# Weight remainders of the expert stage: three quarters on VectorE, one quarter on GpSimd, and two weight loads released from a wait

## The chip, the cores and the metric

The kernel runs on one core of one Trainium2 chip. The metric is the device time of one execution in microseconds (us); the medians here are over a few executions of the same program. A core has TensorE (PE in the rows; PEld is its weight load), VectorE (DVE), ScalarE (ACT), GpSimd (POOL) and SyncE (SP), each with its own queue that is worked off strictly in order; they wait for one another by semaphores. SP issues most DMAs, POOL issues the indirect ones (gathers and scatters).

## The reference

Three layers run one after the other: an attention with heads mixed before and after the softmax, a dense layer, and a layer of eight experts with one expert per token. The change lies in the third.

```
xn = x / (norm(x) + 1e-6); en = expert_emb / (norm(expert_emb) + 1e-6)
logits = xn @ en.T / tau
expert_idx = argmax(logits, axis=1)          # 1792 tokens, 8 experts
gate_w = softmax(logits)[token, expert_idx]
for e in range(8):
    mask = expert_idx == e
    h = maximum(x[mask] @ w1[e], 0)          # 768 -> 1024
    out[mask] = gate_w[mask] * (h @ w2[e])   # 1024 -> 768
```

Everything is float32 in and out.

## The kernel before

Products are made from 16-bit pieces: a float32 operand is split into a high part (float16) and a remainder (bfloat16, the float32 value less its high part), and three matmuls (high by high, remainder by high, high by remainder) are added up in PSUM.

**The expert stage** (`moe2`, `one_round`) goes through nine lists of tokens. List 0 holds the first 276 tokens of the fullest expert and starts while the dense layer is still ending; lists 1 to 7 hold the other experts, at most 306, 276, 224, 208, 208, 192 and 160 tokens; list 8 is the rest of the fullest expert, 64 tokens. A list is eight units. For unit (e, f) one DMA of 768 KB brings a tile `wr` with 128 rows of the first weight (j = 0) and of the second (j = 1), out of six buffers (`fetch`, L870 to L876). `split` (L892 on) makes the high part `wh` on ScalarE (L902) and the remainder `wl` (L903), 128x768 each; these have three buffers for each j. `first` multiplies the list's tokens with the first weight (18 matmuls, L913), applies the relu (ScalarE writes `rh`, L917; VectorE writes `rl` from PSUM, L918); `second`, two units later, multiplies with the second weight (18 matmuls, L937). After a list's last unit its sums are copied out (`ot`, L947 on VectorE and L949 on ScalarE), transposed on TensorE (L966), scaled by the gate (`or`, L971, VectorE) and scattered to the output by GpSimd (L974).

The tokens of a list come as rows: SP loads the list's indices `ids` (L833), GpSimd gathers the rows `xr` out of the DRAM table `yg` (L839), TensorE transposes them (L854), ScalarE and VectorE write the two pieces `xph` (L858) and `xpl` (L859, from PSUM). The gather for list e+1 is issued at unit (e, 0). These transposes, the units' first products and the output transposes take turns in two PSUM banks.

**Between dense layer and list 1** stands the routing of the last 256 tokens: their sums are copied (`yt`, L569), logits taken, the expert picked and placed (L598 to L648), the rows normalised and written to `yg` (L698), the counts of the experts ranked (L725 to L739). Only then can list 1 be gathered. List 0's remainders are kept for list 8 (`kept_xl`, the same line L903), so list 8 needs none.

**The order.** Lines are written in the order of the loops; a scheduler that follows dependencies moves them on each engine's queue. SP issues the weight DMAs ahead as far as `PF` = 5 units reach and buffers are free; the DMA of unit (1, 0) waits besides, by a dependency written by hand (L873), until the gathered rows of list 1 have landed, and SP being in order, those of (1, 1) and so on stand behind it.

Of the kernel before, what the change touches and what calls it, by code (L numbers as in the profile page):

```python
# [17 lines left out]
ALU = mybir.AluOpType  # L18
# [782 lines left out]
def moe2(tc, ctx, bank, ident, yg, pos, keep, ids0, chosen, w12, out, before):  # L801
    nc = tc.nc
# [22 lines left out]
    def one_round(lists, wins, offs, nm, before=None):  # L825
# [44 lines left out]
        def fetch(e, f):  # L870
            raw = p4.tile([128, 2, DM], F32, tag="wr", name=f"wr_{nm}_{e}_{f}")
            s = nc.sync.dma_start(out=raw, in_=w12[bass.ds(lists[e][0], 1), f].rearrange("o p j d -> (o p) j d"))
            if before and (e, f) == (1, 0):  # L873
                tc.add_manual_dep(s.ins, gathered[-1].ins.name,
                                  mybir.DependencyInfo(mybir.DependencyClass.Sync, mybir.DependencyReason.DATA),
                                  reason="the gathered rows are needed before these weights")  # L876
            for j in range(2):
                RW[e, f, j] = raw[:, j]

        def lasting(f, j):  # L880

            if (f, j) not in kept:
                p, n = (chosen["pool"], 4) if f < 4 else (late["w"], 2 * MF - 8)
                t = [p.tile([128, CC, 512] if f < 4 else [128, n * DM], dt, tag=tag, name=f"kept_{tag}_{f}")
                     for dt, tag in ((F16, "xh"), (BF, "xl"))]
                if f < 4:
                    t = [x.rearrange("p a b -> p (a b)") for x in t]
                for k in range(n):
                    kept[f + k // 2, k % 2] = tuple(x[:, k * DM:(k + 1) * DM] for x in t)
            return kept[f, j]  # L890

        def split(e, f, j):  # L892
            if wins[e] == LATE:
                RW[e, f, j] = kept[f, j]
                return
            raw = RW[e, f, j]
            if before and e == 0:
                wh, wl = lasting(f, j)
            else:
                wh = p3.tile([128, DM], F16, tag=f"wh{j}", name=f"wh{j}_{nm}_{e}_{f}")  # L900
                wl = p3.tile([128, DM], BF, tag=f"wl{j}", name=f"wl{j}_{nm}_{e}_{f}")
            nc.scalar.copy(wh, raw)  # L902
            (nc.vector if j else nc.gpsimd).tensor_tensor(out=wl, in0=raw, in1=wh, op=ALU.subtract)  # L903
            RW[e, f, j] = (wh, wl)

        def first(e, f):
# [76 lines left out]
        def fetch_to(i):  # L983
            while ahead and units.index(ahead[0]) <= i and ahead[0][0] < len(lists):
                fetch(*ahead.pop(0))

        fetch_to(0)
        gather(0, *((ids0, 1 + BLOCKS[-1][0]) if before else ()))
        fetch_to(PF - 1)
        split(0, 0, 0)  # L990
        split(0, 0, 1)
        for c in range(3):
            if before:
# [5 lines left out]
        for i, (e, f) in enumerate(units):  # L999
# [3 lines left out]
            if i + 1 < len(units):  # L1003
                with ExitStack() as order:
                    if before and i < 3:
                        order.enter_context(tc.issue_after(chosen["hl" if i < 2 else "rows"].ins))
                    split(*units[i + 1], 0)
                    split(*units[i + 1], 1)
# [145 lines left out]
```

## Time and profile before

| | us |
|---|---|
| median of 3 executions (lowest, highest) | 1286.94 (1285.57, 1294.75) |
| the profiled execution, its own time | 1288.26 |
| its span, first to last instruction | 1286.0 |
| TensorE busy in the span | 1193.8 |
| VectorE, ScalarE, GpSimd busy | 855.1, 729.0, 707.3 |
| expert stage, lists 1 to 8 and the end | about 1029 to 1286 of the span |

How to read it: all times in the rows are counted from the start of the span. "Busy" is the time in which an engine has an instruction running, including time for which that instruction is held up. A share over the whole span mixes three layers; the rows that follow are therefore cut by stretches.

### The profile page before, as it was taken

Reading aid. Unit: us, or ns where it says so; the run is one execution under the profiler, and the core shown is the slowest. Engines: PE = TensorE matmul, PEld = TensorE weight load, DVE = VectorE, ACT = ScalarE, POOL = GpSimd, SP = SyncE. Lnnn points to the kernel's source line nnn. Section 1 sums busy time; section 2 is a strip of 40 time slices with the busy share of each in tenths; the row PEclk is TensorE's granted clock in tenths of the full one; section 3 lists DMA queues with packets and bytes.
Section 4 is the critical chain, followed back from the end, with each engine's and each line's share of the span. In section 5 each row is a group of like instructions: output and inputs, shape, how many; then the busy total and the mean of one; then the engine's idle time right before and its main releaser. Section 6 shows DMA issues by size and latency. Waiting matters only on the chain.

```text
span 1286.0 us, 23742 instructions
## 1 busy us (share of the span) xinstructions
PE 1193.8 (93%) x8624; PEld 837.4 (65%) x8648; DVE 855.1 (66%) x1895; ACT 729.0 (57%) x1499; POOL 707.3 (55%) x594
## 2 busy tenths in 40 slices
PE   8999899989999988999899999999978899999995
PEld 3655565555555664566566666667876678989883
DVE  5877687768767829977766456745878345566662
ACT  6777687667767744444455444545556334555551
POOL 5887678577767753433443335334566355566550
PEclk8999999999999999999999999999998999999998
DMA  6555746555574476223001000100043656678640
GB/s 212 174 182 146 221 162 190 175 182 184 148 208 162 116 236 219 93 97 131 25 1 50 1 25 1 50 1 1 2 140 133 212 194 205 213 242 263 229 159 22
DMA packets 82854, 173.90 MB, mean 135 GB/s; under 512 B 12155, under 2 KB 60155, under 8 KB 82728
## 3 DMA queue, kind: packets, MB, share of 16 engines
q1 hardware_dynamic: 76986, 160.75, 38.7%
q0 software_dynamic: 5472, 11.43, 3.0%
q8 instruction: 70, 1.15, 0.4%
q14 instruction: 56, 0.46, 0.1%
q10 hardware_dynamic: 270, 0.12, 0.0%
HBM read 110.79 MB, written 23.30 MB: 104 GB/s over the span
## 4 chain that ended last, share of the span: by engine, by line
PE 59%; DVE 16%; DMA 12%; ACT 6%; issue 3%; POOL 2%; SPq 0%; POOLq 0%; ACTq 0%; DVEq 0%
PE bank L561 11%; PE bank L533 10%; PE bank L913 7%; PE bank L240 7%; PE bank L937 7%; PE bank L290 7%; DMA G<-S 3%; PE bank L203 3%; DMA raw_v<-in_v_dram 3%; PE bank L305 2%; DVE g L547 2%; DMA wor<-in_w_out_dram 2%; DVE g L548 2%; DVE wl_a L903 2%; ACT A L250 1%
## 5 line engine op out<-in xcount | busy, mean ns | idle before, releaser
L561 PE MATMUL bank<-ghl,whl 128*128 128x512 f32 (+1 forms) x1152 | 258.1, 376 | 9.3 <-POOL ghl L551 4.9
L561 PEld LDWEIGHTS bank<-ghl,whl 128*128 128x128 f32 x1152 | 199.6, 192 | 50.8 <-POOL ghl L551 6.3
L483 POOL TENSOR_TENSOR whl<-wo,whl 128x768 fp32r<-128x768 f32 x64 | 118.8, 1857 | 177.2 <-ACT whl L482 177.1
L295 POOL TENSOR_TENSOR at<-at 128x480 f16<-128x480 f32 x180 | 177.0, 996 | 51.9 <-ACT at L294 50.2
L240 PE MATMUL bank<-G,wmix 120*120 120x448 f32 x360 | 176.7, 575 | 11.3 <-DMA G<-S 11.3
L290 PE MATMUL bank<-wr,A 120*128 120x120 f32 (+4 forms) x1800 | 175.3, 246 | 5.2 <-ACT x L312 3.0
L250 ACT ACTIVATE A<-bank,st 120x448 f32<-120x448 f32 x180 | 114.3, 636 | 53.5 <-DVE st L244 22.2
L244 DVE TENSOR_REDUCE st<-bank 120x1 f32<-120x448 f32 x180 | 111.2, 618 | 46.3 <-PE bank L240 45.1
L903 POOL TENSOR_TENSOR wl_a<-wr_a,wh_a 128x768 bf16<-128x768 f32 x56 | 93.1, 1670 | 70.4 <-ACT wh_a L902 70.0
L551 POOL TENSOR_TENSOR ghl<-g,ghl 128x512 fp32r<-128x512 f32 (+1 forms) x64 | 76.6, 1197 | 99.7 <-ACT ghl L550 99.7
L903 DVE TENSOR_TENSOR wl_a<-wr_a,wh_a 128x768 bf16<-128x768 f32 x56 | 83.1, 1484 | 61.9 <-ACT wh_a L902 61.9
L533 PEld LDWEIGHTS <-wih 128*128 128x128 f16 x768 | 72.4, 99 | 76.3 <-issue 15.9
L290 PEld LDWEIGHTS bank<-wr,A 120*128 120x128 f32 (+1 forms) x720 | 94.5, 198 | 34.5 <-issue 17.8
L294 ACT COPY at<-bank 128x480 f32<-128x480 f32 x180 | 101.3, 567 | 25.0 <-PE bank L290 24.7
L902 ACT CAST wh_a<-wr_a 128x768 f16<-128x768 f32 x112 | 92.6, 829 | 39.2 <-PE bank L937 35.2
L543 DVE SCALAR_TENSOR_TENSOR g<-bank,u 128x512 f32<-128x512 f32 (+1 forms) x64 | 39.9, 623 | 108.6 <-ACT d L540 105.2
L255 POOL TENSOR_TENSOR A<-A 120x448 f16<-120x448 f32 (+1 forms) x90 | 84.4, 938 | 32.0 <-ACT A L250 13.4
L482 ACT CAST whl<-wo 128x768 fp32r<-128x768 f32 x64 | 53.1, 831 | 71.1 <-PE bank L561 53.0
L533 PE MATMUL bank<-mxh,wih 128*128 128x512 f16 (+1 forms) x384 | 85.1, 358 | 5.4 <-DVE d L544 4.2
L290 PEld LDWEIGHTS <-A 120*128 120x128 bf16 (+2 forms) x1080 | 63.1, 100 | 40.9 <-issue 33.9
L550 ACT CAST ghl<-g 128x512 fp32r<-128x512 f32 (+1 forms) x64 | 36.2, 566 | 91.6 <-DVE g L548 81.0
L913 PE MATMUL bank<-xph_a,wh_a 128*128 128x208 f16 (+5 forms) x336 | 87.2, 262 | 0.0
(214 smaller groups left out, 2701.3 us busy)
## 6 DMA issues: line engine op xcount, KB each, us to landing
wr_a<-in_w_dram SPq DMA_DIRECT2D x64, 768.0 KB
G<-S SPq DMA_DIRECT2D x176, 210.0 KB
raw_w<-in_w_in_dram SPq DMA_DIRECT2D x32, 384.0 KB
wor<-in_w_out_dram SPq DMA_DIRECT2D x16, 768.0 KB
raw_v<-in_v_dram SPq DMA_DIRECT2D x16, 384.0 KB
yg<-row SPq DMA_DIRECT2D x3, 1540.0 KB
raw_q<-in_q_dram SPq DMA_DIRECT2D x9, 448.0 KB
raw_k<-in_k_dram SPq DMA_DIRECT2D x9, 448.0 KB
```

What stands on the lines that cost most here:

```text
L240: nc.tensor.matmul(ps[:r, :S], wmix[:r, :r], g[:r], start=True, stop=True)
L244: nc.vector.tensor_reduce(out=st[:r, k:k + 1], in_=ps[:r, :S], axis=AX.X, op=ALU.min)
L250: nc.scalar.activation(out=a[:r, :S], in_=ps[:r, :S], func=AF.Exp, bias=bias, scale=-1.0, accum_out=st[:r, 4 + k:5 + k])
L290: nc.tensor.matmul(ps[:, jc * r:jc * r + r], x[:r, js], w[:r].rearrange("p (a b) -> p a b", b=10)[:, :, :n], start=(i == 0), stop=(i == le ...
L294: nc.scalar.copy(at32[:, :, t0:t0 + n], v)
L295: nc.gpsimd.tensor_tensor(out=atl[:, :, t0:t0 + n], in0=at32[:, :, t0:t0 + n], in1=ath[:, :, t0:t0 + n], op=ALU.subtract)
L483: nc.gpsimd.tensor_tensor(out=w[:, 1], in0=wo[f], in1=w[:, 0].bitcast(F32), op=ALU.subtract)
L533: nc.tensor.matmul(h, u[f][:, c], X[b][v][:, c, :N], start=(i == 0), stop=(i == len(seq) - 1))
L561: nc.tensor.matmul(Y[b][c][:, :N], w[:, u, 128 * c:128 * c + 128], hl[:, v, :N], start=(f == 0 and i == 0), stop=(f == FC - 1 and i == 2))
L902: nc.scalar.copy(wh, raw)
L903: (nc.vector if j else nc.gpsimd).tensor_tensor(out=wl, in0=raw, in1=wh, op=ALU.subtract)
L913: nc.tensor.matmul(h, w[u][:, 128 * c:128 * c + 128], XP[e][v][:, c, :N], start=(i == 0), stop=(i == len(seq) - 1))
```

## The change

The remainders were made on VectorE for the second weight (j = 1) and on GpSimd for the first (j = 0). Now GpSimd makes them where f + 2j is a multiple of four: the first weight of units 0 and 4 and the second weight of units 2 and 6, four of a list's sixteen; VectorE makes the other twelve. The dependency on the gathered rows moves from the DMA of unit (1, 0) to that of unit (1, 2).

```diff
@@ fetch
-            if before and (e, f) == (1, 0):
+            if before and (e, f) == (1, 2):
                 tc.add_manual_dep(s.ins, gathered[-1].ins.name,
@@ split
             nc.scalar.copy(wh, raw)
-            (nc.vector if j else nc.gpsimd).tensor_tensor(out=wl, in0=raw, in1=wh, op=ALU.subtract)
+            (nc.gpsimd if (f + 2 * j) % 4 == 0 else nc.vector).tensor_tensor(out=wl, in0=raw, in1=wh, op=ALU.subtract)
```

The scheduler's queues change at these places. In the names, `wl0_a_4_3` is the remainder of the first weight (j = 0) of list 4, unit 3; `xr_a_5_0` is a third or half of list 5's rows.

GpSimd's queue about the gather for list 5, which is issued while list 4 begins; before:

```order
L903 TENSOR_TENSOR wl0_a_4_1_13046<-wr_a_4_1_12794,wh0_a_4_1_13045 128x768
L903 TENSOR_TENSOR wl0_a_4_2_13097<-wr_a_4_2_12862,wh0_a_4_2_13096 128x768
L839 DMA xr_a_5_0_13041<-yg_61,ids_a_5_13039 104x770
L839 DMA xr_a_5_1_13043<-yg_61,ids_a_5_13039 104x770
L903 TENSOR_TENSOR wl0_a_4_3_13161<-wr_a_4_3_12920,wh0_a_4_3_13160 128x768
L903 TENSOR_TENSOR wl0_a_4_4_13232<-wr_a_4_4_12986,wh0_a_4_4_13231 128x768
L903 TENSOR_TENSOR wl0_a_4_5_13291<-wr_a_4_5_13037,wh0_a_4_5_13290 128x768
L974 DMA out_0_dram<-or_a_3_0_13152,oi_a_3_0_12479 1792x768
```

and now:

```order
L903 TENSOR_TENSOR wl0_a_4_0_12989<-wr_a_4_0_12729,wh0_a_4_0_12988 128x768
L903 TENSOR_TENSOR wl1_a_3_6_12869<-wr_a_3_6_12594,wh1_a_3_6_12868 128x768
L839 DMA xr_a_5_0_13041<-yg_61,ids_a_5_13039 104x770
L839 DMA xr_a_5_1_13043<-yg_61,ids_a_5_13039 104x770
L903 TENSOR_TENSOR wl0_a_4_4_13232<-wr_a_4_4_12986,wh0_a_4_4_13231 128x768
L903 TENSOR_TENSOR wl1_a_4_2_13101<-wr_a_4_2_12862,wh1_a_4_2_13100 128x768
L974 DMA out_0_dram<-or_a_3_0_13152,oi_a_3_0_12479 1792x768
L974 DMA out_0_dram<-or_a_3_1_13223,oi_a_3_1_12483 1792x768
```

Behind the gather stand two remainders instead of three before the scatter, and one of the two belongs to the second weight.

VectorE's queue at the same place, from the relu remainder `rl` of unit (4, 1) on; before:

```order
L918 SCALAR_TENSOR_TENSOR rl_a_4_1_13124<-bank7_828_13104,rh_a_4_1_13123 128x208
L947 COPY ot_a_3_13145<-bank1_810_12700 128x224
L947 COPY ot_a_3_13145<-bank3_812_12702 128x224
L947 COPY ot_a_3_13145<-bank5_814_12704 128x224
L971 TENSOR_SCALAR or_a_3_0_13152<-bank6_829_13153,gate_a_3_0_12478 112x384
L903 TENSOR_TENSOR wl1_a_4_2_13101<-wr_a_4_2_12862,wh1_a_4_2_13100 128x768
L918 SCALAR_TENSOR_TENSOR rl_a_4_2_13188<-bank7_830_13168,rh_a_4_2_13187 128x208
L971 TENSOR_SCALAR or_a_3_0_13152<-bank6_831_13191,gate_a_3_0_12478 112x384
```

and now:

```order
L918 SCALAR_TENSOR_TENSOR rl_a_4_1_13124<-bank7_828_13104,rh_a_4_1_13123 128x208
L947 COPY ot_a_3_13145<-bank1_810_12700 128x224
L947 COPY ot_a_3_13145<-bank3_812_12702 128x224
L947 COPY ot_a_3_13145<-bank5_814_12704 128x224
L971 TENSOR_SCALAR or_a_3_0_13152<-bank6_829_13153,gate_a_3_0_12478 112x384
L918 SCALAR_TENSOR_TENSOR rl_a_4_2_13188<-bank7_830_13168,rh_a_4_2_13187 128x208
L971 TENSOR_SCALAR or_a_3_0_13152<-bank6_831_13191,gate_a_3_0_12478 112x384
L903 TENSOR_TENSOR wl0_a_4_5_13291<-wr_a_4_5_13037,wh0_a_4_5_13290 128x768
```

The remainder that stood ahead of `rl` of unit (4, 2) is gone from VectorE; the next one stands behind it.

VectorE's queue between list 0 and list 1, from `rl` of unit (0, 4) to the fourth of the six pieces `xpl` of list 1; before:

```order
L918 SCALAR_TENSOR_TENSOR rl_a_0_4_11300<-bank6_745_11280,rh_a_0_4_11299 128x276
L918 SCALAR_TENSOR_TENSOR rl_a_0_5_11347<-bank7_746_11327,rh_a_0_5_11346 128x276
L918 SCALAR_TENSOR_TENSOR rl_a_0_6_11394<-bank6_747_11374,rh_a_0_6_11393 128x276
L859 TENSOR_TENSOR xpl_a_1_11398<-bank7_748_11399,xph_a_1_11397 128x306
L903 TENSOR_TENSOR wl1_a_1_0_11436<-wr_a_1_0_11225,wh1_a_1_0_11435 128x768
L859 TENSOR_TENSOR xpl_a_1_11398<-bank6_749_11423,xph_a_1_11397 128x306
L903 TENSOR_TENSOR wl1_a_1_1_11531<-wr_a_1_1_11274,wh1_a_1_1_11530 128x768
L918 SCALAR_TENSOR_TENSOR rl_a_0_7_11459<-bank7_750_11439,rh_a_0_7_11458 128x276
L859 TENSOR_TENSOR xpl_a_1_11398<-bank6_751_11462,xph_a_1_11397 128x306
L903 TENSOR_TENSOR wl1_a_1_2_11582<-wr_a_1_2_11321,wh1_a_1_2_11581 128x768
L859 TENSOR_TENSOR xpl_a_1_11398<-bank7_752_11486,xph_a_1_11397 128x306
```

and now:

```order
L918 SCALAR_TENSOR_TENSOR rl_a_0_4_11300<-bank6_745_11280,rh_a_0_4_11299 128x276
L903 TENSOR_TENSOR wl1_a_1_0_11436<-wr_a_1_0_11225,wh1_a_1_0_11435 128x768
L918 SCALAR_TENSOR_TENSOR rl_a_0_5_11347<-bank7_746_11327,rh_a_0_5_11346 128x276
L903 TENSOR_TENSOR wl0_a_1_1_11527<-wr_a_1_1_11274,wh0_a_1_1_11526 128x768
L903 TENSOR_TENSOR wl1_a_1_1_11531<-wr_a_1_1_11274,wh1_a_1_1_11530 128x768
L918 SCALAR_TENSOR_TENSOR rl_a_0_6_11394<-bank6_747_11374,rh_a_0_6_11393 128x276
L859 TENSOR_TENSOR xpl_a_1_11398<-bank7_748_11399,xph_a_1_11397 128x306
L903 TENSOR_TENSOR wl0_a_1_2_11578<-wr_a_1_2_11321,wh0_a_1_2_11577 128x768
L859 TENSOR_TENSOR xpl_a_1_11398<-bank6_749_11423,xph_a_1_11397 128x306
L918 SCALAR_TENSOR_TENSOR rl_a_0_7_11459<-bank7_750_11439,rh_a_0_7_11458 128x276
L859 TENSOR_TENSOR xpl_a_1_11398<-bank6_751_11462,xph_a_1_11397 128x306
L859 TENSOR_TENSOR xpl_a_1_11398<-bank7_752_11486,xph_a_1_11397 128x306
```

Of the three remainders that stood among the pieces `xpl` one is left; three others stand ahead of them.

On SP's queue nothing changes its place: the write of `yg`, the indices of list 1, then the DMAs of units (1, 0), (1, 1), (1, 2), of which the third now carries the wait for the rows.

## Rows read from the trace of the kernel before

**Rows 1.** The page, busy us of each engine, share of the span, instructions.

```profile
PE 1193.8 (93%) x8624; PEld 837.4 (65%) x8648; DVE 855.1 (66%) x1895; ACT 729.0 (57%) x1499; POOL 707.3 (55%) x594
```

**Rows 2.** Busy time by stretch: length, each engine's us and (count), granted clock, DMA share, GB/s.

```profile
1015.00:1029.00 14.00, 11.03 (x80) 8.55 (x81) 7.84 (x9) 6.95 (x13) 5.39 (x3) 0.88 0.92 366
1029.00:1140.00 111.00, 111.00 (x982) 95.49 (x981) 58.41 (x107) 53.19 (x94) 60.01 (x40) 1.00 0.64 210
1140.00:1256.00 116.00, 107.24 (x1215) 104.61 (x1213) 77.44 (x116) 62.61 (x115) 67.91 (x44) 0.97 0.66 215
```

**Rows 3.** The same by stretches of 4 us, inside lists 4 to 7.

```profile
1148.00:1152.00 4.00, 1.20 (x12) 1.05 (x12) 3.89 (x5) 0.78 (x1) 2.08 (x3) 1.00 0.17 45
1208.00:1212.00 4.00, 1.53 (x9) 1.43 (x10) 3.62 (x5) 0.15 (x1) 2.07 (x2) 0.82 0.21 30
1212.00:1216.00 4.00, 4.00 (x38) 3.88 (x37) 1.68 (x3) 1.14 (x3) 0.97 (x2) 0.75 0.93 339
1232.00:1236.00 4.00, 2.43 (x29) 2.04 (x26) 4.00 (x3) 2.62 (x7) 2.70 (x2) 1.00 0.28 51
1236.00:1240.00 4.00, 3.19 (x28) 3.10 (x29) 3.47 (x9) 1.02 (x2) 0.00 (x0) 0.74 0.91 350
1240.00:1244.00 4.00, 4.00 (x48) 3.98 (x47) 2.04 (x5) 1.52 (x3) 2.59 (x2) 0.84 0.20 55
```

**Rows 4.** Waits of TensorE from 920 us on: us in total, times, longest.

```profile
PE bank L966 <- DVE rl_a L918: 6.1, 3, 3.1
...
PE bank L854 <- DMA xr_a<-yg,ids_a: 3.2, 3, 1.3
PE bank L854 <- DVE xpl_a L859: 3.2, 3, 1.6
PE bank L966 <- DVE ot_a L947: 2.3, 1, 2.3
```

**Rows 5.** Timeline of GpSimd at list 4: start, us, what.

```profile
1144.77 4.86 POOL L903 TENSOR_TENSOR wl_a<-wr_a,wh_a 128x768 bf16<-128x768 f32 x3
```

**Rows 6.** Timeline of VectorE at the same place.

```profile
1141.61 0.96 DVE L903 TENSOR_TENSOR wl_a<-wr_a,wh_a 128x768 bf16<-128x768 f32 x1 [1.74 <-ACT wh_a L902]
...
1145.03 5.42 DVE L903 TENSOR_TENSOR wl_a<-wr_a,wh_a 128x768 bf16<-128x768 f32 x1
```

**Rows 7.** Line L903 in the whole span: ns shortest/median/longest, first and last start.

```profile
L903 POOL TENSOR_TENSOR wl_a<-wr_a,wh_a x56: 1637/1647/2173, 1020.1 to 1247.7; 128x768 bf16<-128x768 f32 x56
L903 DVE TENSOR_TENSOR wl_a<-wr_a,wh_a x56: 942/1204/5453, 1020.8 to 1254.2; 128x768 bf16<-128x768 f32 x56
...
L903 DVE TENSOR_TENSOR kept_xl<-wr_a,kept_xh x8: 943/1414/1787, 969.5 to 991.9; 128x768 bf16<-128x768 f32 x8
```

**Rows 8.** Groups of 1140 to 1256 us: count, busy us, mean ns, idle before.

```profile
L903 DVE TENSOR_TENSOR wl_a<-wr_a,wh_a 128x768 bf16<-128x768 f32 x31 | 49.8, 1607 | 30.1 <-ACT wh_a L902 30.1
...
L903 POOL TENSOR_TENSOR wl_a<-wr_a,wh_a 128x768 bf16<-128x768 f32 x29 | 48.0, 1669 | 26.1 <-ACT wh_a L902 25.9
```

**Rows 9.** Timeline of SP between list 0 and list 1.

```profile
998.50 0.38 SPq L698 DMA_DIRECT2D yg<-row  x1
1001.59 0.33 SPq L833 DMA_DIRECT2D ids_a<-pos  x1
1015.06 3.30 SPq L872 DMA_DIRECT2D wr_a<-in_w_dram  x6
```

**Rows 10.** The chain of waits there: start, us, what.

```profile
998.50 6.92 DMA yg<-row
...
1009.29 5.65 DMA xr_a<-yg,ids_a
...
1016.25 8.20 DMA wr_a<-in_w_dram
```

**Rows 11.** Timeline of the routing stretch, GpSimd and VectorE.

```profile
976.89 9.51 POOL L903 TENSOR_TENSOR kept_xl<-wr_a,kept_xh 128x768 bf16<-128x768 f32 x5
976.97 3.20 DVE L866 COPY gate_a<-xr_a 92x2 f32<-92x2 f32 x3
```

## The prediction

> **What bounds the kernel now.** I read the page first, then stretches, then who waits inside them. Over the whole span TensorE is busy 93% [rows 1], so there are some 92 us without it, and the question is which of them the change can reach. It touches only the expert stage and the routing before it. There the stretches differ [rows 2]. From 1029 to 1140 us (lists 1 to 3 and the start of list 4) TensorE is busy 111.00 of 111 us at the full clock: no rearrangement of remainders can gain anything there, and none costs anything as long as they stay ahead. From 1140 to 1256 it is busy 107.24 of 116 us, at a granted clock of 0.97. The finer cut [rows 3] shows that its 8.76 us of idleness lie in a few holes, the large ones in 1148 to 1152, 1208 to 1212 and 1232 to 1240, where lists 4, 6 and 7 have just begun, and that the clock is lower behind the second and third (0.82 and 0.75; 0.74 and 0.84).
>
> Who makes the holes? Of TensorE's waits, 6.1 us in three pieces are for `rl`, VectorE's relu remainder, and 2.3 us for `ot` [rows 4]. Neither is long work. The timelines show what stands ahead of them: GpSimd, held up until then by the gather for the next list, makes three remainders in a row, 4.86 us [rows 5]; VectorE's remainder of the second weight, begun 0.26 us later, takes 5.42 us, though the one before took 0.96 [rows 6]. While GpSimd's three run, VectorE's one does not advance; `rl`, behind it on VectorE, is late, a PSUM bank is not freed, and TensorE stands. Line L903 as a whole says the same: on VectorE 0.94 us at best, 5.45 at worst, on GpSimd always about 1.65 [rows 7].
>
> Ahead of list 1 the chain is another one: the write of `yg`, the gather, and the weights, which SP issues at 1015.06, only after the rows have landed [rows 9, 10]. TensorE waits 3.2 us for the rows and about 3 for `xpl` [rows 4], which stands on VectorE behind remainders that wait for those weights.
>
> **The change, part by part.** *Lists 4 to 7, holes.* At list 4 the remainder that was held 5.42 us moves to GpSimd, behind the gather; VectorE comes to `rl` directly, and its next remainder stands behind `rl`. GpSimd has two remainders in a row there instead of three: 2 x 1.65 = 3.3 us. The pattern is the same in every list, since it depends on f and j alone. Neither of the two is needed at once: their products come about two units later. So the 8.76 us of holes can go. *Clock.* Of full-speed time the low clock costs (1 - 0.82 + 1 - 0.75) x 4 = 1.7 us behind one hole and (0.26 + 0.16) x 4 = 1.7 us behind the other, together 3.4 us [rows 3]; with no hole there is no low clock. That is 12.2 us. I keep back 1.0 us, since VectorE now has two remainders in many units and `ot` could be late by some tenths in list 7: **-11.2 us**. The bounds are -12.2, and 0 if the holes only move.
>
> *Lists 1 to 3.* Nothing on the path; the cover is TensorE's own 111 us, against VectorE's 58.41 and GpSimd's 60.01 [rows 2]. 12 rests a list instead of 8 at 0.94 us add less than 4 us a list to VectorE, and GpSimd loses 4 x 1.65.
>
> *Routing.* For list 0 VectorE gets four remainders more, 4 x 0.94 = 3.8 us, on the chain that ends with the write of `yg` at 998.50. That is the upper bound. Against it stands the holding of today: three tiny copies `gate` took 3.20 us beside a run of five remainders on GpSimd of 9.51 us [rows 11], and the eight kept remainders have a median of 1.41 instead of 0.94 us [rows 7], 8 x 0.47 = 3.8 us. With GpSimd's run down to three, most of that could go: the lower bound is 3.8 - 3.2 - 3.8 = -3.2 us. I take **+1.5 us**, nearer the upper end, because two of VectorE's new remainders stand ahead of the `gate` copies in time and one of GpSimd's stays beside them.
>
> *Two weight loads earlier.* On SP the DMAs of (1, 0) and (1, 1) stand behind the indices of list 1, so they leave at about 1002 instead of 1015 [rows 9]. Their 1.57 MB need 4.3 us at the 366 GB/s of the stretch from 1015 on [rows 2]. They meet the end of the `yg` write (until 1005.42) and are over when the gather's last part goes (1009.29) [rows 10]; between 0 and 4.3 us of delay I take **+0.7 us**, as most of the write is ahead of them in the same queue. The gain is that of the three remainders that stood among the pieces `xpl` two stand ahead of them now, and can run while TensorE and VectorE wait for the rows anyway; one, that of (1, 2), stays, and its weight leaves as late as that of (1, 0) today. Of the 3 us waited for `xpl` I credit **-2.5 us**; the bounds are 0 and -3. Everything else behind it (ScalarE's high parts, the other four weights) comes earlier or as now. These three give -0.3 us.
>
> *Sum.* -11.2 - 0.3 = -11.5 us. Against the profiled execution, 1288.26 us, that is 1276.8; the median of the runs is 1.3 us lower, so **1275.4 us**, 0.9% less. One per cent, 12.9 us (1274.1), is about what a measurement of this kernel tells from no change; the forecast lies just inside it.
>
> **Rivals.**
>
> *The holes halve.* GpSimd's pair behind the gather, 3.3 us, still holds a VectorE remainder, and something that TensorE wants stands behind it. For: the gather still blocks GpSimd for several us. Against: the queue has `rl` ahead of that remainder. Half of 12.2 gives -6.1, with -0.3: 1280.5 us.
>
> *One shared path.* If the two engines can never work at L903 at once, their sum counts: a list costs 8 x 1.65 + 8 x 0.94 = 20.7 us today and 4 x 1.65 + 12 x 0.94 = 17.9 us then, 2.8 us less. It could bound only the shortest of the large lists, list 7; then the other holes stay and the gain is 2.8 us: 1284.1 us. The Trainium skill (Perfetto Trace Analysis, Optimizing Scalar/DVE Operations) says that the two share an SBUF read port, so that moving work between them might not help. By that rule, this case; the trace agrees that they hold each other up [rows 5, 6], but shows the price in bursts and not in sums.
>
> *Everything goes.* All 12.2 us, the rows of list 1 not later, and 3.0 us at `xpl`: -15.2, 1271.7 us. For: holding in the routing stretch may fall more than I credit.
>
> *Slower: VectorE becomes the bound of lists 4 to 7.* It has 77.44 us of work from 1140 on, of which 49.8 are 31 remainders at a mean of 1.607 us [rows 2, 8]; of the 60 there it would make 45. At today's mean that is 27.6 + 45 x 1.607 = 99.9 us, against 107.24 - 3.4 = 103.8 us of TensorE at full clock: just hidden. At 0.94 us it is 69.9. The point from which it decides is a mean of (116 - 27.6)/45 = 1.96 us; at 2.2 us the stretch takes 126.6, 10.6 us more: 1297.5 us. Against: GpSimd, the cause of the long ones, has half the work (15 of 60 instead of 29).
>
> **Chances and range.** The forecast 0.42, the holes halved 0.23, one shared path 0.10, everything 0.18, slower 0.07. The forecast's own range, with the routing and the loads between their bounds, is 1272 to 1279. Four fifths reach over the first two cases, part of the third and most of the fourth: 1270 to 1285 us. Faster by over 1% means below 1274.1: nearly all of "everything" and some 0.4 of the forecast, 0.35. Slower by over 1% is the end of the slow case: 0.04. Within 1%: 0.61.
>
> **What would show it.** Right: from 1140 us (shifted) on TensorE idle below 1.5 us and the clock at 1.00 up to list 8; VectorE's longest remainder below about 3.5 us and its mean near 1.1; no row "L966 <- `rl`"; the write of `yg` 0 to 3 us later, the gather landing 1 to 4 us later; `wr` of (1, 0) landed before the rows. Wrong: a new wait of TensorE for `wl` itself on L913 or L937, or for the rows by more than 7 us; VectorE busy above 95% in list 7; or holes that stay at the same places although GpSimd's runs are short, for then the gather and not the run of three made them.

## The result, and the profile after

| | before | after |
|---|---|---|
| median, us (lowest to highest of 4 executions each) | 1288.12 (1285.57 to 1294.75) | 1271.99 (1271.26 to 1276.81) |
| ratio after to before, 95% interval | | 0.9875 (0.983 to 0.992) |
| the profiled execution, us | 1288.26 | 1272.35 |
| its span, us | 1286.0 | 1270.1 |

The change made the kernel 1.25% faster. The forecast was 1275.4 us, the range 1270 to 1285. The time lies in the range, 3.4 us below the forecast and 0.3 us from the rival "everything goes" (1271.7). The forecast started from a median of 1286.94 us and took off 11.5; from 1288.12 the change took off 16.1.

Where did 15.9 us of the two profiled executions go? The page answers to [rows 1]: TensorE has 4.7 us less busy time and 81.0 us without work instead of 92.2.

```profile
PE 1189.1 (94%) x8648; PEld 832.9 (66%) x8648; DVE 857.8 (68%) x1927; ACT 728.2 (57%) x1499; POOL 656.4 (52%) x562
```

More is seen from list 1's first product with remainders of its own (L913) to list 8's first product (L930). Columns as in [rows 2]; this is the kernel before, in full, which the rows on record showed in two pieces:

```profile
1029.00:1260.60 231.60, 222.84 (x2288) 204.63 (x2286) 137.67 (x229) 117.12 (x213) 127.91 (x84) 0.99 0.63 209
```

And the changed kernel:

```profile
1025.80:1243.90 218.10, 218.10 (x2289) 201.67 (x2286) 138.08 (x256) 117.21 (x213) 87.64 (x57) 1.00 0.67 218
```

TensorE's idle time there goes from 231.60 - 222.84 = 8.76 us to none. The same products take 222.84 - 218.10 = 4.74 us less, together 13.5 us. Of the 4.74 us the clock accounts for 3.4: it is now 1.00, the upper of its two levels (2.4 GHz), from end to end; before, it was lower only in the stretches of [rows 3] at and behind two of the three large holes, after TensorE had stood. In steps of 4 us it was 1.00 everywhere else from 1140 to 1256 us. The other 1.3 us is taken up further down. VectorE's busy time is the same although it carries out 27 instructions more: what it had spent on being held up it now spends on work.

The place of [rows 5, 6] in the changed kernel, GpSimd's timeline first:

```profile
1140.37 3.25 POOL L903 TENSOR_TENSOR wl_a<-wr_a,wh_a 128x768 bf16<-128x768 f32 x2
```

and VectorE's (start, us, what, and the idle time ahead):

```profile
1139.84 0.88 DVE L947 COPY ot_a<-bank 128x224 f32<-128x224 f32 x2
...
1143.20 0.38 DVE L918 SCALAR_TENSOR_TENSOR rl_a<-bank,rh_a 128x208 bf16<-128x208 f32 x1 [1.36 <-ACT rh_a L917]
1143.50 0.61 DVE L971 TENSOR_SCALAR or_a<-bank,gate_a 112x384 f32<-112x384 f32 x1
1144.02 0.95 DVE L903 TENSOR_TENSOR wl_a<-wr_a,wh_a 128x768 bf16<-128x768 f32 x1
```

While GpSimd has its two remainders, VectorE reads PSUM (`ot`, `rl`, `or`) and is not disturbed; its next remainder starts when GpSimd's run is over and takes 0.95 us instead of 5.42. Line L903 as a whole, against [rows 7]:

```profile
L903 DVE TENSOR_TENSOR wl_a<-wr_a,wh_a x84: 940/958/3206, 1006.9 to 1237.5; 128x768 bf16<-128x768 f32 x84
...
L903 POOL TENSOR_TENSOR wl_a<-wr_a,wh_a x28: 1634/1644/1682, 1008.9 to 1234.8; 128x768 bf16<-128x768 f32 x28
L903 DVE TENSOR_TENSOR kept_xl<-wr_a,kept_xh x12: 943/948/1768, 966.1 to 990.0; 128x768 bf16<-128x768 f32 x12
```

VectorE's median fell from 1204 to 958 ns, and for list 0's remainders from 1414 to 948. TensorE's waits from 920 us on, against [rows 4]: `rl`, `ot` and the two late `xpl` are gone, the wait for the gathered rows has grown from 3.2 to 5.0 us.

```profile
PE bank L854 <- DMA xr_a<-yg,ids_a: 5.0, 3, 2.6
```

SP between the lists, against [rows 9]: the six weight loads are now one row that begins behind the indices, and it lasts until the rows are there, as the third of them waits.

```profile
996.61 0.38 SPq L698 DMA_DIRECT2D yg<-row  x1
998.66 0.33 SPq L833 DMA_DIRECT2D ids_a<-pos  x1
999.24 16.52 SPq L872 DMA_DIRECT2D wr_a<-in_w_dram  x6
```

The whole span by stages, in us, from the starts of a few lines in each profile: *dense*, the dense layer's first product (L533), counted from the span's start; *write*, from the dense layer's last weight load (L561) to the last write of `yg` (L698); *list 1*, from there to list 1's first product with a remainder of its own (`wl`, L913); *lists*, from there to list 8's first product (L930); *end*, to the span's end. What lies between *dense* and *write* was 513.5 to 518.4 us in all fourteen profiles and is left out.

| kernel | dense | write | list 1 | lists | end | median (runs) | ratio to before (95%) |
|---|---|---|---|---|---|---|---|
| before | 463.0 | 19.9 | 30.5 | 231.6 | 25.4 | 1288.12 (4) | |
| the change | 459.7 | 19.4 | 29.2 | 218.1 | 26.2 | 1271.99 (4) | 0.9875 (0.983, 0.992) |
| e1 rule only | 463.1 | 19.4 | 28.3 | 218.1 | 26.2 | 1277.06 (7) | 0.9903 (0.987, 0.994) |
| e2 dependency only | 466.2 | 19.9 | 30.8 | 231.8 | 25.4 | 1290.03 (12) | 1.0003 (0.997, 1.004) |
| e3 other units | 460.1 | 19.3 | 29.4 | 228.5 | 25.0 | 1283.41 (12) | 0.9957 (0.993, 0.998) |
| e4 unit 2 swapped | 462.0 | 19.4 | 28.4 | 221.9 | 25.2 | 1275.40 (6) | 0.9900 (0.986, 0.994) |
| e5 change again | 460.9 | 19.4 | 28.0 | 218.1 | 26.1 | 1269.71 (6) | 0.9883 (0.985, 0.991) |
| e6 all on VectorE | 461.6 | 19.4 | 29.4 | 219.4 | 25.3 | 1270.37 (6) | 0.9899 (0.987, 0.993) |
| e7 doubles | 462.8 | 19.3 | 31.1 | 240.0 | 25.0 | 1296.72 (6) | 1.0098 (1.006, 1.013) |
| e8 rule in lists only | 457.1 | 19.9 | 29.4 | 218.1 | 25.3 | 1269.63 (6) | 0.9890 (0.986, 0.992) |
| e9 fills, blurred | 461.5 | 19.4 | 28.8 | 243.1 | 25.9 | 1293.64 (12) | 1.0034 (1.001, 1.006) |
| e10 dependency at (1, 5) | 464.7 | 19.4 | 33.9 | 218.1 | 26.3 | 1281.61 (10) | 0.9941 (0.992, 0.996) |
| e11 rule only again | 463.6 | 19.4 | 28.6 | 218.2 | 26.2 | 1271.56 (6) | 0.9870 (0.984, 0.990) |
| e12 fills alone | 464.8 | 19.3 | 30.4 | 220.3 | 24.7 | 1274.94 (6) | 0.9883 (0.985, 0.992) |

The column *dense* varies by 9 us although no kernel differs there: medians of a few runs can differ by some us for that reason alone. The column *lists* is the same within 0.2 us wherever the list code is the same. So the stage columns decide, and the ratios confirm. Each ratio is to executions of the kernel before on the same chip; e1 to e4 share those, so do e5 to e8 and e9 to e11.

### The profile page after: what moved, and what is told of

The parts are those of the page before. It is cut to its first block, busy times and chain, and to the rows that moved or that the text cites. A ratio compares the mean times of both kernels' runs of the same rounds, so it can differ in the third digit from the quotient of the medians.

```text
span 1270.1 us, 23774 instructions
## 1 busy us (share of the span) xinstructions
PE 1189.1 (94%) x8648; PEld 832.9 (66%) x8648; DVE 857.8 (68%) x1927; ACT 728.2 (57%) x1499; POOL 656.4 (52%) x562
## 4 chain that ended last, share of the span: by engine, by line
PE 62%; DVE 13%; DMA 12%; ACT 5%; issue 3%; POOL 2%; SPq 0%; POOLq 0%; ACTq 0%; DVEq 0%
PE bank L561 12%; PE bank L533 10%; PE bank L937 9%; PE bank L913 8%; PE bank L240 8%; PE bank L290 7%; DMA G<-S 4%; PE bank L203 3%; DMA raw_v<-in_v_dram 3%; DMA wor<-in_w_out_dram 2%; PE bank L305 2%; DVE g L547 2%; DVE g L548 2%; DVE wo L81 1%; DVE wo L79 1%
## 5 line engine op out<-in xcount | busy, mean ns | idle before, releaser
L561 PE MATMUL bank<-ghl,whl 128*128 128x512 f32 (+1 forms) x1152 | 258.7, 377 | 10.6 <-POOL ghl L551 4.8
L561 PEld LDWEIGHTS bank<-ghl,whl 128*128 128x128 f32 x1152 | 200.1, 192 | 52.2 <-POOL ghl L551 6.2
L533 PEld LDWEIGHTS <-wih 128*128 128x128 f16 x768 | 72.7, 99 | 76.3 <-issue 15.9
L903 DVE TENSOR_TENSOR wl_a<-wr_a,wh_a 128x768 bf16<-128x768 f32 x84 | 83.0, 990 | 33.3 <-ACT wh_a L902 33.1
L533 PE MATMUL bank<-mxh,wih 128*128 128x512 f16 (+1 forms) x384 | 85.1, 358 | 5.3 <-DVE d L544 3.8
L937 PE MATMUL bank<-rh_a,wl_a 128*128 128x208 f16 (+5 forms) x336 | 86.2, 260 | 0.0
L937 PE MATMUL bank<-rl_a,wh_a 128*128 128x208 bf16 (+5 forms) x336 | 86.2, 260 | 0.0
```

The lines of the kernel that those rows point to most:

```text
L533: nc.tensor.matmul(h, u[f][:, c], X[b][v][:, c, :N], start=(i == 0), stop=(i == len(seq) - 1))
L561: nc.tensor.matmul(Y[b][c][:, :N], w[:, u, 128 * c:128 * c + 128], hl[:, v, :N], start=(f == 0 and i == 0), stop=(f == FC - 1 and i == 2))
L937: nc.tensor.matmul(O[e][c][:, :N], w[u][:, 128 * c:128 * c + 128], r[v], start=(f == 0 and i == 0), stop=(f == MF - 1 and i == 2))
```

## The experiments

Each edit is shown against the changed kernel, with `...` for what is left out. In the expectations "theory" is the account in the prediction, as the runs so far had left it, and "rival" another account that would give other numbers. A remainder is *held* when it takes much longer than 0.95 us on VectorE, and a *hole* is a stretch in which TensorE stands idle.

**e1, the rule without the moved dependency.**

```diff
-            if before and (e, f) == (1, 2):
+            if before and (e, f) == (1, 0):
```

> The quarter rule without the moved dependency. Theory (the holes of lists 4 to 7 came from VectorE's remainder held up by a run on GpSimd; the moved dependency is worth about nothing): no wait of TensorE on L966 for rl, TensorE without a hole from list 4 to list 8 (114.7 us as with the whole change, 128.1 before), and about 1273 us. Rival (the dependency carries part of the gain, as the other three loads of list 1 and with them xpl come earlier): list 1's first product 2 to 3 us later than with the whole change, counted from the dense layer's last product, and 1275 or more.

All 13.5 us of the lists are there, and the start of list 1 is not later than with the whole change (28.3 against 29.2 and 28.0). The median, 1277.06, is above the theory's 1273 and where the rival had it (1275 or more), but its executions spread from 1271.27 to 1282.18; e11, the same kernel again, had 1271.56 and settles it. TensorE's wait for `xpl` fell from 3.2 to 0.5 us without the moved loads:

```profile
PE bank L854 <- DMA xr_a<-yg,ids_a: 3.5, 3, 1.4
...
PE bank L854 <- DVE xpl_a L859: 0.5, 1, 0.5
```

**e2, the dependency alone,** with the old rule:

```diff
-            (nc.gpsimd if (f + 2 * j) % 4 == 0 else nc.vector).tensor_tensor(
+            (nc.vector if j else nc.gpsimd).tensor_tensor(
```

> The moved dependency with the old rule (GpSimd j = 0, VectorE j = 1). Theory: the holes of lists 4 to 7 stay as they were (lists 4 to 8 again take about 128 us), the start of list 1 moves by less than 2 us; 1286 to 1288 us. Rival (the dependency carries part of the gain): list 1 starts 2 to 3 us earlier, 1284 to 1285. If the program's first 930 us, which no part of the change touches, again end some 3 us earlier than in the profile of before, that difference belongs to the run and not to the change.

Nothing gained: lists 231.8, list 1 at 30.8, ratio 1.0003. The median, 1290.03, lies above both expectations, and *dense* was 3 us longer than in the profile of before. The waits:

```profile
PE bank L966 <- DVE rl_a L918: 6.3, 3, 3.1
PE bank L854 <- DMA xr_a<-yg,ids_a: 5.1, 3, 2.7
...
PE bank L966 <- DVE ot_a L947: 2.3, 1, 2.3
PE bank L854 <- DVE xpl_a L859: 1.9, 2, 1.7
```

What `xpl` gives back (3.2 to 1.9) the rows take (3.2 to 5.1).

**e3, a quarter on GpSimd, but other units.**

```diff
-            (nc.gpsimd if (f + 2 * j) % 4 == 0 else nc.vector)
+            (nc.gpsimd if ((f, j) in ((1, 0), (2, 0), (3, 0), (6, 0)) if e else (f + 2 * j) % 4 == 0) else nc.vector)
```

> A quarter on GpSimd as in the change, but other units in lists 1 to 7: the first weight of units 1, 2, 3 and 6. So VectorE's remainder of the second weight of unit 2 stands ahead of rl of unit 2 again, as before the change; behind the gather GpSimd has one remainder, not three. Theory (GpSimd's run holds it up): it takes at most 1.65 + 0.96 = 2.6 us, no hole over 1 us, 1272 to 1275 us. Rival (it is the place of that remainder ahead of rl that makes the hole, whatever GpSimd does): waits L966 for rl of some 6 us again, lists 4 to 8 take 124 us or more, 1281 us or more.

A miss for the theory as I had put it: it allowed a hold of 2.6 us and no hole over 1 us. The held remainders took 2.7 to 2.9 us at lists 4 to 6 and 4.38 us at list 7, behind two of GpSimd's, and the holes came back: 10.4 us in the lists against the change, and 1283.41 us, which is the rival's time. The line over the span, then VectorE and GpSimd at list 4:

```profile
L903 DVE TENSOR_TENSOR wl_a<-wr_a,wh_a x84: 941/958/4378, 1005.3 to 1247.3; 128x768 bf16<-128x768 f32 x84
```

```profile
1139.42 0.38 DVE L947 COPY ot_a<-bank 128x224 f32<-128x224 f32 x1
1139.85 2.90 DVE L903 TENSOR_TENSOR wl_a<-wr_a,wh_a 128x768 bf16<-128x768 f32 x1
1142.67 0.68 DVE L947 COPY ot_a<-bank 128x224 f32<-128x224 f32 x2
```

```profile
1140.25 1.68 POOL L903 TENSOR_TENSOR wl_a<-wr_a,wh_a 128x768 bf16<-128x768 f32 x1
```

One GpSimd remainder, behind the gather, stretches VectorE's from 0.95 to 2.90 us. This one, the first weight of unit 4, used to be GpSimd's and now stands between the copies `ot`; so `ot` and `or` are late, and TensorE waits for them:

```profile
PE bank L966 <- DVE or_a L971: 6.2, 4, 2.2
...
PE bank L966 <- DVE ot_a L947: 1.0, 1, 1.0
```

The rival's story isn't right either: nothing waits for `rl` of unit 2. It is not the share, and not one fixed place; what counts is whether a held remainder has something behind it that TensorE wants at once.

**e4, half on GpSimd, unit 2 exchanged.**

```diff
+            (nc.gpsimd if (j == (f == 2) if e else (f + 2 * j) % 4 == 0) else nc.vector)
```

> Half on GpSimd as before the change, with one exchange in lists 1 to 7: in unit 2 the second weight's remainder goes to GpSimd, the first's to VectorE. So no remainder stands ahead of rl of unit 2 on VectorE, but GpSimd has a run of four behind the gather (6.6 us). Theory (the run holds the next VectorE remainder): the remainder of unit 3 is held instead, 3 to 6 us, with rl of unit 3 behind it; holes of 4 to 9 us stay in lists 4 to 7, one unit later, 1279 to 1288 us. Rival (place ahead of rl of unit 2 alone): no holes, 1272 to 1274 us.

GpSimd's share is that of before and its run even longer, yet most of the gain is there: lists 221.9, 3.8 us more than with the change and 9.7 less than before. GpSimd at list 4, then VectorE:

```profile
1141.00 6.48 POOL L903 TENSOR_TENSOR wl_a<-wr_a,wh_a 128x768 bf16<-128x768 f32 x4
```

```profile
1144.60 0.62 DVE L971 TENSOR_SCALAR or_a<-bank,gate_a 112x384 f32<-112x384 f32 x1 [0.98 <-PE bank L966]
1145.13 3.17 DVE L903 TENSOR_TENSOR wl_a<-wr_a,wh_a 128x768 bf16<-128x768 f32 x1
1148.23 0.36 DVE L918 SCALAR_TENSOR_TENSOR rl_a<-bank,rh_a 128x208 bf16<-128x208 f32 x1
```

As the theory said, unit 3's remainder is held, 3.17 us, until the run ends (1147.48); it did not say that `rl` of unit 3 is needed less urgently. TensorE waits 1.6 us for it in all lists:

```profile
PE bank L913 <- DVE rl_a L918: 1.6, 2, 1.1
```

So the hold was the theory's and the time, 1275.4, nearer the rival's.

**e5, the change again.** No edit.

> The changed kernel once more, to see what of its time repeats. Theory: from list 1's first product to list 8's first product 218 us again (before 231.6, first experiments 218.1, 231.8, 228.5, 221.9), in every profile of this rule; the time ahead of the dense layer's first product, 460 to 466 us in the profiles so far with the same instructions in all of them, varies and carries no part of the change; median 1272 to 1277 us. Rival (the change does something to the first 930 us as well): that stretch ends at 460 us again and the median is 1272 or less.

*Lists* is as the theory said. The rival's two signs came too: *dense* is 460.9, near 460, and the median is below 1272. But *dense* is 463.1, 464.7 and 463.6 in e1, e10 and e11, which have the same rule, and on this chip the kernel before had 1283.73, on that of e1 to e4 1288.10; the ratio is the same as at first (0.9883 against 0.9875). So the lower median is not the change's.

**e6 and e7, all remainders of lists 1 to 7 on VectorE, without and with doubles on GpSimd.**

```diff
-            (nc.gpsimd if (f + 2 * j) % 4 == 0 else nc.vector)
+            (nc.gpsimd if (e == 0 and (f + 2 * j) % 4 == 0) else nc.vector)
 # e7 alone:
+            if e and j == 0:
+                spare = p3.tile([128, DM], BF, tag="spare", bufs=1, ...)
+                nc.gpsimd.tensor_tensor(out=spare, in0=raw, in1=wh, op=ALU.subtract)
```

> In lists 1 to 7 all remainders on VectorE, none on GpSimd; list 0 and the dependency as in the change. A remainder of the first weight of unit 4 then stands between the copies ot, and one of unit 2 ahead of rl, but nothing holds them. Theory (a hole takes both: a remainder ahead of something that TensorE wants at once, and a run on GpSimd that holds it): VectorE's remainders all at about 0.95 us, longest below 2 us outside the gathers; holes of at most 1 us a list; list 1 to list 8 in 218 to 222 us; 1272 to 1278 us. Rival (place alone makes the hole): as with the other quarter, 228 us, 1283 or more. Rival of the prediction (VectorE becomes the bound): VectorE above 95% busy in list 7, TensorE waiting for wl on L913 or L937.

> As the kernel with all remainders on VectorE, and GpSimd computes those of the first weight of lists 1 to 7 a second time into a tile that nobody reads. VectorE's instructions are the same in the same order; nothing waits for GpSimd's results. Theory (GpSimd's runs hold VectorE's remainders up by themselves): remainders of 3 to 6 us on VectorE at the lists' starts, waits on L966 for ot, or or rl, list 1 to list 8 in 228 us or more, 1284 to 1295 us. Rival (what counts is only who makes which remainder and in what order): the same as without the doubles within 2 us.

VectorE's queue is the same in both, and nothing waits for the doubles' results. Without them the remainder between the copies `ot` that cost e3 its holes takes 0.96 us at most, TensorE waits 0.7 us in all lists, and the time is that of the change. With them the lists take 20.6 us more, the kernel 2%, somewhat above the 1284 to 1295 us expected, although the longest remainder is 3.23 us, at the lower end of what was expected. The line in e6, over the span, and its wait from 1030 us on:

```profile
L903 DVE TENSOR_TENSOR wl_a<-wr_a,wh_a x112: 943/957/960, 1003.9 to 1237.0; 128x768 bf16<-128x768 f32 x112
...
PE bank L966 <- DVE or_a L971: 0.7, 3, 0.3
```

and the groups of e7 between list 1 and list 8 (count, busy us, mean ns, idle before), with its waits:

```profile
L903 DVE TENSOR_TENSOR wl_a<-wr_a,wh_a 128x768 bf16<-128x768 f32 x106 | 152.2, 1449 | 14.1 <-ACT wh_a L902 13.7
L906 POOL TENSOR_TENSOR spare_a<-wr_a,wh_a 128x768 bf16<-128x768 f32 x53 | 104.8, 1978 | 41.2 <-ACT wh_a L902 20.5 <-issue 19.0 <-POOL spare_a L906 0.6
```

```profile
PE bank L969 <- DVE or_a L974: 7.4, 7, 2.4
PE bank L854 <- DVE xpl_a L859: 5.8, 4, 2.7
```

Both engines lose: VectorE has 1449 ns in the mean where e6 had 957 at the median and 960 at the longest, GpSimd 1978 where it has some 1645 with the change. All of TensorE's waits in the lists are for VectorE, none for weights. VectorE does not become the bound even with all of it: in e6 it is busy 16.19 us of the 20 us from 1218 on, in list 7 (columns as in [rows 2]).

```profile
1218.00:1238.00 20.00, 19.77 (x263) 18.81 (x261) 16.19 (x28) 11.78 (x25) 2.46 (x2) 1.00 0.39 125
```

**e8, the rule in lists 1 to 7 alone,** dependency as before:

```diff
-            if before and (e, f) == (1, 2):
+            if before and (e, f) == (1, 0):
-            (nc.gpsimd if (f + 2 * j) % 4 == 0 else nc.vector)
+            (nc.gpsimd if ((f + 2 * j) % 4 == 0 if e else j == 0) else nc.vector)
```

> The quarter rule in lists 1 to 7 alone; list 0 and the dependency as before the change. Theory: list 1 to list 8 in 218 us; from the write of yg to list 1's first product 28 to 29 us (30.5 before, 28.3 with the rule in all lists), since the wait for xpl goes with the remainders of list 1, not with those of list 0; from the dense layer's last product to the write of yg 19.9 us as before, where the rule in list 0 too has 19.4. 1273 to 1277 us. Rival (list 0's four remainders gave the gain ahead of list 1): 30 us or more from the write to the first product.

Lists 218.1 and *write* 19.9 as expected; the median, 1269.63, is below the 1273 to 1277 expected, the ratio, 0.9890, that of the change. List 1 at 29.4 lies between the two expectations; the wait for `xpl` (0.6 us) speaks for the theory. List 0's part of the rule is worth 0.5 us ahead of the write: 19.9 in the three kernels with the old rule there, 19.3 or 19.4 in the eleven others.

**e9 and e12, GpSimd fills a spare tile with zeros instead of subtracting.** In e9 ScalarE writes one column first so that the fill waits; in e12 GpSimd copies one column itself and fills twice. Both have the rule of e6.

```diff
 # e9
+            if e and j == 0:
+                spare = p3.tile([128, DM], BF, tag="spare", bufs=3, ...)
+                nc.scalar.copy(spare[:, :1], raw[:, :1])
+                nc.gpsimd.memset(spare, 0.0)
 # e12
+            if e and j == 0:
+                spare = p3.tile([128, DM], BF, tag="spare", bufs=1, ...)
+                nc.gpsimd.tensor_copy(spare[:, :1], wh[:, :1])
+                for _ in range(2):
+                    nc.gpsimd.memset(spare, 0.0)
```

> As the doubles, but GpSimd only fills the spare tile with zeros (it writes and reads nothing; ScalarE writes one column first, so that each fill waits for its unit). Theory (it is GpSimd's reading that holds VectorE's remainders): remainders at 0.95 us as with all on VectorE and no doubles, list 1 to list 8 in 219 to 222 us, 1269 to 1275 us. Rival (any work of GpSimd beside them holds them, or its place in the schedule does): remainders of 2 us and more, 228 us or more, 1280 or more.

The time, 1293.64, is the rival's, the remainders (958 ns median, 986 at most) are the theory's. The waits tell why: the column had put ScalarE behind the loads.

```profile
ACT spare_a L906 <- DMA wr_a<-in_w_dram: 60.3, 35, 6.6
```

The experiment measured its own flaw and decides nothing about the time; so once more:

> The fills once more, without ScalarE's part in them, which had made ScalarE wait for the weights (60.3 us in that kernel) and so blurred its time: GpSimd copies one column of the unit's high part, so as to wait for it, and fills the spare tile twice, about 1.5 us of writing at the places where the doubles stood. VectorE's instructions stand as with all on VectorE. Theory (only GpSimd's reads hold VectorE's remainders): none above 1.1 us, list 1 to list 8 in 219 to 222 us, 1269 to 1276 us, against 240.0 us and 1296.7 with the doubles. Rival (GpSimd's being busy there costs the time, by late gathers or scatters, and not the holding): 228 us or more, 1280 or more, with remainders at 0.95 us all the same.

The theory's case. VectorE's instructions follow each other from list 1 on in the same order as in e6 and e7. In the lists GpSimd's copies and fills are busy 110 us, about as much as the doubles in e7 (104.8), and no remainder is held, also beside the copy of one column, which reads: 0.99 us at most; lists 220.3.

```profile
L903 DVE TENSOR_TENSOR wl_a<-wr_a,wh_a x112: 944/957/990, 1010.4 to 1245.0; 128x768 bf16<-128x768 f32 x112
```

```profile
L908 POOL MEMSET spare_a<- 128x768 bf16 x106 | 78.3, 739 | 5.7
L906 POOL CAST spare_a<-wh_a 128x1 bf16<-128x1 f16 x53 | 31.7, 597 | 25.6 <-ACT wh_a L902 24.1
```

**e10 and e11, the dependency at (1, 5) and at (1, 0), with the rule.**

```diff
-            if before and (e, f) == (1, 2):
+            if before and (e, f) == (1, 5):     # e11: (1, 0)
```

> The change with the dependency at (1, 5): five of the list's loads need not wait for the rows. Theory (the loads ahead of the gather cost what the rows come later, and give nothing back, as the wait for xpl went with the rule): TensorE's wait for the rows 3.5 us with the dependency at (1, 0), 4.5 to 5.0 at (1, 2), here 6 to 10; from the write of yg to list 1's first product 29 to 34 us (28.3 at (1, 0), 28.0 and 29.2 at (1, 2)); 1272 to 1279. Rival (earlier loads help, as I predicted for two): 27 us or less and 1266 to 1271.

> The rule with the dependency left at (1, 0), again, beside the one with five loads released and with a second profile. Theory: from the write of yg to list 1's first product 28 to 29 us, as with the change within 1 us; ratio to the kernel before 0.987 to 0.991, the same as the change within its interval. Rival (the moved dependency carries part of the gain): 30 us or more and a ratio of 0.992 or more.

TensorE's wait for the rows is 3.5 and 3.8 us with the dependency at (1, 0), 4.5 to 5.0 at (1, 2) with the rule of the change (it and e5), and here:

```profile
PE bank L854 <- DMA xr_a<-yg,ids_a: 10.9, 3, 8.2
```

List 1 is 5 us later and the time 1281.61; both the wait and the time are somewhat above what the theory had (6 to 10 us, 1272 to 1279). Without the moved dependency (e11) the ratio is 0.987, within the interval of the change.

## Why the prediction was right, and where not

**Holes of lists 4 to 7: mechanism right, one term missing.** Forecast -11.2 us, measured -13.5 in every profile of the rule. The idle time went as put, all 8.76 us, and so did the 3.4 us of the clock [rows 3]. The 1.0 us kept back for late `ot` in list 7 was not needed. What the sum had at nothing is the other 1.3 us of TensorE's busy time, which no row of the clock shows. Part of it is how the rows count: in the kernel before, a product's row in list 4 lasts some 250 ns although the next one starts some 90 ns after it, so the last product ahead of a hole counts 0.16 us more as busy. Over the six holes that is 1.0 us, an estimate; the rest stays open. That VectorE's remainders are held by GpSimd's, and that this makes the holes, is shown by e6, e7 and e12. What I had not said, and e3 shows, is that the quarter as such is no cure: which units GpSimd has decides what stands behind a held remainder. My argument by the order at list 4 held for this choice of units.

**Routing: forecast +1.5, measured -0.5** (*write* in the table; e8 keeps 19.9). The sign was wrong. The step that failed is "nearer the upper end": four remainders more at 0.95 us are paid by the holding that ends, median 1414 to 948 ns.

**Two loads earlier: the sum near by luck, the gain put down to the wrong edit.** I credited the moved dependency with -2.5 us at `xpl` and charged +0.7 for later rows, together -1.8; list 1 came 1.3 and 2.5 us earlier (the change, e5). But the rule alone gives as much: 2.2 and 1.9 us in e1 and e11. There and in e8, where the loads are not moved, the wait for `xpl` falls from 3.2 to 0.5, 1.7 and 0.6 us, because of the remainders among the pieces only the first is still held (1.77 us in e1; before, three took 1.77, 2.01 and 1.77). The rows come about 1 us later with two loads ahead of them (the change and e5 against e1 and e11) and, with five, 7. In sum the dependency is worth nothing that these runs can tell: 30.8 against 30.5 us without the rule, 29.2 and 28.0 against 28.3 and 28.6 with it. For routing and loads together I had -0.3, measured are -1.8 and -3.0 (the change, e5).

**The range.** The forecast's own range, 1272 to 1279, is narrower than the bounds that the prediction names for it: with the routing between -3.2 and +3.8 us and the loads between -3 and +4.3 it would run from 1269.5 to 1283.8.

**What is left of the 15.9 us:** -3.3 us ahead of the dense layer and +1.9 in it, in which nothing was changed, so these 1.4 us are chance; +0.8 at the end (26.1 to 26.3 us in five kernels, 24.7 to 25.9 in the others), whose cause stays open.

**Rivals.** "Everything goes" came nearest, by its sum and not by its story, since the rows did come later. The holes did not halve. One shared path: the two do hold each other up at L903, and moving work between them helped all the same: in lists of 31 us on average (218.1 / 7) TensorE hides that where nothing urgent stands behind. The Trainium skill (SBUF — State Buffer, Who interferes with whom) says that a VectorE instruction with two SBUF inputs contends with a GpSimd instruction that reads SBUF and not with one that only writes it; e7 and e12 agree (1449 and 955 ns mean). VectorE as the bound: excluded by e6. On the chances: I gave 0.61 to "within 1%" and 0.35 to faster; 1.25% is just beyond. Of the signs named beforehand, TensorE's idle time, the clock, the longest remainder (3.21 us, ahead of list 1), their mean (0.99 us) and the missing wait for `rl` came as named; the write of `yg` came not later but 0.5 us earlier in its stage.

## What to carry to other kernels

Where a two-input operation on VectorE takes a multiple of its shortest time, GpSimd's reads of SBUF may be holding it up, as here; look at the longest instance and at GpSimd's timeline beside it before balancing shares. Then look at what stands behind the held one on VectorE: a held instruction costs only if something urgent queues behind it, so moving one of them past the urgent one (e4) may do nearly as much as taking half the work off GpSimd. And judge an edit of 1% by the length of the stage it touches, when another stage varies by as much.

## What the runs showed of the hardware that was not expected

- A VectorE remainder is not let in between GpSimd's remainders that follow each other at once: 5.42 us beside a run of three [rows 5, 6], 3.17 us to the end of a run of four (e4). The same page of the Trainium skill (SBUF: two separate sides) says that whoever starts first has the port pair for its whole instruction; that the next GpSimd instruction gets it again ahead of a waiting VectorE one is what these rows add.
- By the rows, starting first did not decide it in e3: at list 4 VectorE's remainder began 0.40 us ahead of GpSimd's and ended 0.82 us after it, and lists 5 and 6 show the same (2.71 and 2.91 us). Each time GpSimd was still issuing a gather when VectorE's began, though in e6 no remainder beside a gather took more than 0.96 us. Spans on GpSimd are rough, so this stays an observation.
- GpSimd's fills, 739 ns for 128x768 bf16, held no remainder of VectorE (0.99 us at most in e12).
